# All low-part subtractions of the expert weights and of the second network's output weights on one engine

## The chip, the cores and the metric

The kernel runs on 1 core of a Trainium2 chip. The metric is the device time of one execution in microseconds (us). Five engines work side by side, each through its own queue in order: PE (TensorE, matrix products), DVE (VectorE), ACT (ScalarE), POOL (GpSimd) and SP (SyncE, which here only issues transfers).

## The reference, cut to what matters

Three stages in a row, all in float32: attention with global tokens, a mixture of experts with one expert per token, and a gated network with a convolution of three taps.

```python
def _moe_ref(x, w_gate, w_local, w1, w2):            # x: 4 x 576 x 512, 8 experts
    ...
            h = np.maximum(x[b, s] @ w1[e], 0.0)     # w1: 8 x 512 x 1024
            out[b, s] = p[e] * (h @ w2[e])           # w2: 8 x 1024 x 512

def _moe2_ref(x, w_in, conv_w, w_out):               # w_in: 512 x 1024, w_out: 1024 x 512
    h = np.maximum(x @ w_in, 0.0)
    ...
    gate = 1.0 / (1.0 + np.exp(-conv_out))
    return (h * gate @ w_out).astype(np.float32)
```

`moe2_w_in`, `moe2_conv_w` and `moe2_w_out` come as 64-bit floats and are made into 32-bit ones in the kernel.

## The kernel before, in words

Each product is taken as a sum of three, with both operands split in a high part (rounded to the format of PE) and a low part (the rest): high x high, high x low, low x high. So each weight matrix is needed twice, as `wh` and `wl`. For a piece of a matrix, `split_k` (lines 1018 to 1021) does this: ACT casts the staged piece `ws` to `wh` (L1020), and another engine subtracts, `wl = ws - wh` (L1021).

A set of tokens that go to one expert is cut into slots of 128. The loop `step` (L1274) works slot by slot: PE multiplies by the first matrix (`hp`, L1084, four row blocks of 128x1024), ACT applies the relu (`hs`, L1249), PE transposes (`hlp`, L1072), ACT and DVE split what was transposed into high and low (`xh` and `xl` for the tokens of the next slot, `gh` and `gl` for the hidden values, L1073 and L1077), and PE multiplies the hidden values of the slot before by the second matrix (`yp`, L1100, eight row blocks of 128x512). ACT copies the result (`ys`, L1253), and POOL scatters it to memory (L1057) and gathers the rows of a later slot (`xs`, L1045).

Where the next slot has another expert, `resplit` (L1268) splits the newly loaded matrix inside a branch that ACT, DVE and POOL take: the first matrix ahead of the next `hp`, the second matrix behind `gl`. SP loads the matrix after that into the stage as soon as the stage has been read (L1013). In the same steps a 64-bit weight of the second network is converted on DVE by seven integer operations (L987 to L992 and L994), with an exact integer addition on POOL between the last two (L993).

The last slot is written out by hand in `last` (L1186): its second matrix is split in two halves of four pieces; between them stand a small copy (`cw`, L1161) and a flag (`esi`, L939, L940), whose buffers PE needs for its transposes. Then the first rows of the second network are scaled on DVE (`fx`, L1333), transposed on PE (`f_tr`, L1340) and split (`f_x0h`, `f_x0l`, L1342 and L1343), interleaved with PE's `yp`, and the first matrix of the second network is split (`wl<-wf`). At the end of `run` (L1183) its second matrix is split: of eight pieces, DVE casts the odd ones (L1020) and ACT the even ones.

Behind that the second network runs per batch and block of 128 hidden values: PE `f` (L1408), ACT relu (`f_hp`, L1432), three taps on ACT and DVE (`fc`, L1425 and L1427), a sigmoid on ACT, the gate on POOL or DVE (`fg`, L1443), `fl` (L1456) on DVE, and the split of the transposed tokens of the next batch (`fxl`, L1375).

Which engine subtracts follows from four tables by the number of the piece: `POOL_K` for the splits in the loop (first matrix: piece 3; second matrix: pieces 1, 3, 5, 7) and for the first matrix of the second network, `POOL_L` for the last slot's second matrix, `POOL_F` for the second network's second matrix. Calls that name an engine, as the splits of the first two matrices during attention do (`nc.gpsimd`, 12 pieces), do not read the tables.

```python
def split_k(self, n, src, k, eng, cp=None):
    h, l = self.t[n][k]
    (cp.tensor_copy if cp else self.nc.scalar.copy)(h, src[n][:, k, :])
    eng.tensor_tensor(l, src[n][:, k, :], h.bitcast(F32), ALU.subtract)

def split(self, n, src, eng=None):
    for k in range(len(self.t[n])):
        self.split_k(n, src, k, eng or (self.nc.gpsimd if k in POOL_K[n] else self.nc.vector))
```

Of the kernel before, what the change touches and what calls it, by code (L numbers as in the profile page):

```python
# [973 lines left out]
SC_DVE = (0, 1, 2, 3)  # L974
PREP_F = ((3, 4, 5, 6), (1, 3, 5, 6), (1, 3, 5, 6))
PREP0 = {0: (0, 1, 12, 13), 3: (5, 2), 4: (6, 3), 5: (7, 4), 6: (8,), 7: (9,)}
POOL_L = (1, 3, 5, 7)
POOL_F = (1, 3, 5)
DVE_F = (1, 3, 5, 7)
POOL_K = {1: (3,), 2: (1, 3, 5, 7)}  # L980


def conv64(nc, raw, out):
# [13 lines left out]
class Weights:  # L997
# [25 lines left out]
# [5 lines that stand above are left out]
class Moe:  # L1028
# [134 lines left out]
    def run(self, cw6, cwr, cw, f2):  # L1163
# [19 lines left out]
        for k in range(NFC):  # L1183
            W.split_k(2, W.f, k, nc.gpsimd if k in POOL_F else nc.vector, nc.vector if k in DVE_F else None)

    def last(self, s, cwr, cw):  # L1186
# [6 lines left out]
        def split(a, b):  # L1193
            for k in range(a, b):
                W.split_k(1, W.f, k, nc.gpsimd if k in POOL_K[1] else nc.vector)

        def resplit(a, b):
            with self.tc.If(self.chg[s] != 0):
                for k in range(a, b):
                    W.split_k(2, W.s, k, nc.gpsimd if k in POOL_L else nc.vector)  # L1200

# [515 lines left out]
```

## Time and profile before

| what | value |
|---|---|
| median of 3 runs | 684.91 us (684.05 to 686.07) |
| the profiled execution | 682.78 us |
| its span, first to last instruction | 681.0 us |
| mean granted clock of PE | 0.976 of full speed |
| busy: PE, DVE, ACT, POOL | 617.3 us (91%), 435.8 us (64%), 332.6 us (49%), 271.1 us (40%) |
| subtractions `wl<-ws,wh` (L1021) on DVE | 49, 72.6 us in all |
| the same on POOL | 47, 83.0 us in all |

Attention and routing last to about 210 us of the span, the loop over the expert slots to about 450, the last slot to 472, and the second network to the end. A number such as 64% is a mean over these stages; what an engine's time is worth has to be read stage by stage. An engine is "idle before" an instruction when it waits, and the trace names what ended the wait.

### The profile page before, as it was taken

How to read it: one execution, taken by the hardware profiler on the slowest of the kernel's cores; microseconds unless marked ns; L12 is line 12 of the kernel's file. 1: busy time of each engine (PE TensorE's matmuls, PEld its weight loads, DVE VectorE, ACT ScalarE, POOL GpSimd, SP SyncE). 2: the span in 40 equal slices, each digit the busy share in tenths (PEclk: the TensorE clock that was granted, in tenths of full speed). 3: DMA queues.
4: the chain of work that ended last, by engine and by line, in shares of the span. 5: the costliest groups of instructions: out<-in, count | busy, mean ns of one | idle time of the engine just before them, and what ended most of it. 6: DMA issues, size and time to landing. Idle time of an engine off the chain costs nothing. (4 is left out here: it accounts for less than half of the span.)

```text
span 681.0 us, 15354 instructions
## 1 busy us (share of the span) xinstructions
PE 617.3 (91%) x5898; PEld 515.1 (76%) x5898; DVE 435.8 (64%) x824; ACT 332.6 (49%) x634; POOL 271.1 (40%) x281
## 2 busy tenths in 40 slices
PE   8777797787989999799999979986979999999997
PEld 7666675665768878687887868765978898898886
DVE  7866476674855677975767797567986366363340
ACT  5653448865124544452455444563655354363341
POOL 7583810038123545664455556333445142200200
PEclk9999898899799999999999999988979999999999
DMA  9997752354047465546336564321110010000001
GB/s 233 202 236 171 197 136 67 103 205 157 16 140 251 171 229 195 192 179 231 109 148 225 186 219 160 121 97 39 45 46 32 32 63 32 32 16 32 32 32 46
DMA packets 59354, 86.06 MB, mean 126 GB/s; under 512 B 25358, under 2 KB 33830, under 8 KB 59240
## 3 DMA queue, kind: packets, MB, share of 16 engines
q1 hardware_dynamic: 55752, 74.77, 35.3%
q0 software_dynamic: 3520, 10.23, 4.4%
q8 instruction: 48, 0.79, 0.5%
q14 instruction: 34, 0.28, 0.1%
HBM read 125.87 MB, written 15.79 MB: 208 GB/s over the span
## 5 line engine op out<-in xcount | busy, mean ns | idle before, releaser
L1427 DVE SCALAR_TENSOR_TENSOR fc<-f_hp,cw,fc 128x544 f32<-128x544 f32 (+2 forms) x66 | 57.4, 870 | 70.7 <-ACT fc L1425 69.4
L1021 POOL TENSOR_TENSOR wl<-ws,wh 128x512 fp32r<-128x512 f32 (+1 forms) x47 | 83.0, 1793 | 33.0 <-ACT wh L1020 17.1
L1021 DVE TENSOR_TENSOR wl<-ws,wh 128x512 fp32r<-128x512 f32 (+1 forms) x49 | 72.6, 1523 | 6.0 <-ACT wh L1020 5.9
L1100 PE MATMUL yp<-wh,gh 128*128 128x512 f32 x176 | 72.4, 411 | 1.1 <-ACTq L1271 1.1
L1100 PE MATMUL yp<-wl,gh 128*128 128x512 f32 x176 | 69.8, 397 | 0.1
L1100 PE MATMUL yp<-wh,gl 128*128 128x512 f32 x176 | 69.9, 397 | 0.0
L1020 ACT CAST wh<-ws 128x512 fp32r<-128x512 f32 (+1 forms) x96 | 66.1, 777 | 0.0
L1249 ACT ACTIVATE hs<-hp 128x512 f32<-128x512 f32 x44 | 24.3, 595 | 84.4 <-PE hp L1084 84.3
L1084 PE MATMUL hp<-wl,xh 128*128 128x512 f32 x176 | 57.0, 397 | 8.5 <-DVE wl L1021 6.8
L1084 PE MATMUL hp<-wh,xh 128*128 128x512 f32 x176 | 58.6, 405 | 0.7 <-ACT xh L1073 0.7
L1084 PE MATMUL hp<-wh,xl 128*128 128x512 f32 x176 | 56.0, 391 | 0.0
L1485 PE MATMUL f<-wh,fh 128*128 128x512 f32 (+1 forms) x144 | 55.5, 385 | 0.0
L1485 PE MATMUL f<-wl,fh 128*128 128x512 f32 (+1 forms) x144 | 55.0, 382 | 0.0
L1485 PE MATMUL f<-wh,fl 128*128 128x512 f32 (+1 forms) x144 | 55.0, 382 | 0.0
L1045 POOL DMA_INDIRECT xs<-x_dram,gidx x22 | 28.4, 1289 | 52.5 <-ACT pr L274 41.4
L1077 DVE TENSOR_TENSOR gl<-hlp,gh 128x512 fp32r<-128x512 f32 x44 | 28.5, 684 | 31.4 <-ACT gh L1073 27.3
L274 ACT ACTIVATE pr<-sp,nm 128x128 f32<-128x128 f32 x128 | 36.5, 375 | 24.4 <-DVE nm L271 24.4
L1057 POOL DMA_INDIRECT y_dram<-ys,sidx x22 | 25.6, 1165 | 56.5 <-ACT ys L1253 18.9
L1084 PEld LDWEIGHTS hp<-wl,xh 128*128 128x128 f32 x176 | 32.3, 188 | 19.0 <-DVE wl L1021 9.3
L993 POOL TENSOR_TENSOR wf<-wf,fx 128x512 int32<-128x512 int32 x16 | 20.7, 1296 | 62.9 <-DVE fx L992 62.9
L1253 ACT COPY ys<-yp 128x512 f32<-128x512 f32 x22 | 12.9, 586 | 61.2 <-PE yp L1100 56.4
L1100 PEld LDWEIGHTS yp<-wh,gh 128*128 128x128 f32 x176 | 33.9, 192 | 7.9 <-ACTq L1271 1.4
(361 smaller groups left out, 1574.4 us busy)
## 6 DMA issues: line engine op xcount, KB each, us to landing
ws<-in_moe_w_dram SPq DMA_DIRECT2D x42, 2048.0 KB
fx<-y_dram SPq DMA_DIRECT2D x17, 256.0 KB
x_dram<-x SPq DMA_DIRECT2D x16, 256.0 KB
fx<-in_moe_w_in_dram SPq DMA_DIRECT2D x8, 512.0 KB
fx<-in_moe_w_out_dram SPq DMA_DIRECT2D x8, 512.0 KB
out_dram<-fy SPq DMA_DIRECT2D x16, 256.0 KB
VA<-in_v_l_dram SPq DMA_DIRECT2D x20, 192.0 KB
raw<-in_q_l_dram SPq DMA_DIRECT2D x3, 1024.0 KB
```

The source lines that it names most:

```text
L274: nc.scalar.activation(pr[:, hp, :], sp[:, hp, :], AF.Exp, bias=nm[:, hp:hp + 1], scale=-1.0)
L993: nc.gpsimd.tensor_tensor(a, a, lo, ALU.add)
L1020: (cp.tensor_copy if cp else self.nc.scalar.copy)(h, src[n][:, k, :])
L1021: eng.tensor_tensor(l, src[n][:, k, :], h.bitcast(F32), ALU.subtract)
L1045: self.nc.gpsimd.indirect_dma_start(out=xs, out_offset=None, in_=self.x_dram[0:n, :], in_offset=bass.IndirectOffsetOnAxis(ap=self.rt.gidx[ ...
L1057: self.nc.gpsimd.indirect_dma_start(out=self.y_dram[:, :], out_offset=bass.IndirectOffsetOnAxis(ap=self.rt.sidx[:, s:s + 1], axis=0), in_= ...
L1077: self.nc.vector.tensor_tensor(hl[1][:, a:a + 4], t, hl[0][:, a:a + 4].bitcast(F32), ALU.subtract)
L1084: self.nc.tensor.matmul(hp[c], a[:, k, :], b[:, 512 * c:512 * c + 512], start=k == 0 and m == 0, stop=k == NKC - 1 and m == 2)
L1100: self.nc.tensor.matmul(yp, a[:, k, :], b, start=k == 0 and m == 0, stop=k == NFC - 1 and m == 2)
L1249: self.nc.scalar.activation(hs[:, 512 * c:512 * c + 512], hp[c], AF.Relu)
L1427: nc.vector.scalar_tensor_tensor(c[:, a:b], hp[:, a + t:b + t], self.cw[:, t, f:f + 1], c[:, a:b], ALU.mult, ALU.add)
L1485: self.nc.tensor.matmul(yp[:, cs], x[:, c], w[:, cs], start=f == 0 and n == 0, stop=f == NFC - 1 and n == 2)
```

## The change

All tables that name POOL become empty, so all these subtractions go to DVE, in the order of the pieces. Casts, matrix products, loads and branches stay.

```diff
-POOL_L = (1, 3, 5, 7)
-POOL_F = (1, 3, 5)
+POOL_L = ()
+POOL_F = ()
 DVE_F = (1, 3, 5, 7)
-POOL_K = {1: (3,), 2: (1, 3, 5, 7)}
+POOL_K = {1: (), 2: ()}
```

On DVE, in a step of the expert loop, before: from the branch behind `gl` to the first operation of the conversion (`ws_2711` is the stage of the second matrix, the number behind `wl_` the piece).

```order
L1271 COMPARE_AND_BRANCH
L1021 TENSOR_TENSOR wl_0_2721<-ws_2711,wh_0_2720 128x512
L1021 TENSOR_TENSOR wl_2_2725<-ws_2711,wh_2_2724 128x512
L1021 TENSOR_TENSOR wl_4_2729<-ws_2711,wh_4_2728 128x512
L1021 TENSOR_TENSOR wl_6_2733<-ws_2711,wh_6_2732 128x512
L1271 UNCONDITIONAL_BRANCH x2
L987 TENSOR_SCALAR wf_3947<-fx 128x512
```

The same place on DVE now:

```order
L1271 COMPARE_AND_BRANCH
L1021 TENSOR_TENSOR wl_0_2721<-ws_2711,wh_0_2720 128x512
L1021 TENSOR_TENSOR wl_1_2723<-ws_2711,wh_1_2722 128x512
L1021 TENSOR_TENSOR wl_2_2725<-ws_2711,wh_2_2724 128x512
L1021 TENSOR_TENSOR wl_3_2727<-ws_2711,wh_3_2726 128x512
L1021 TENSOR_TENSOR wl_4_2729<-ws_2711,wh_4_2728 128x512
L1021 TENSOR_TENSOR wl_5_2731<-ws_2711,wh_5_2730 128x512
L1021 TENSOR_TENSOR wl_6_2733<-ws_2711,wh_6_2732 128x512
L1021 TENSOR_TENSOR wl_7_2735<-ws_2711,wh_7_2734 128x512
L1271 UNCONDITIONAL_BRANCH x2
L987 TENSOR_SCALAR wf_3947<-fx 128x512
```

Four pieces have come from POOL's queue into DVE's, ahead of the conversion. The first matrix has the same form: its piece 3, which POOL did, now stands behind pieces 0 to 2.

On DVE, in the last slot, from the second half of the second matrix to the first rows of the second network (the difference; `wf_3947` holds the second network's first matrix):

```order
 L1198 COMPARE_AND_BRANCH
 L1021 TENSOR_TENSOR wl_4_2729<-ws_2711,wh_4_2728 128x512
-L1021 TENSOR_TENSOR wl_6_2733<-ws_2711,wh_6_2732 128x512
+L1021 TENSOR_TENSOR wl_5_2731<-ws_2711,wh_5_2730 128x512
+L1021 TENSOR_TENSOR wl_6_2733<-ws_2711,wh_6_2732 128x512
+L1021 TENSOR_TENSOR wl_7_2735<-ws_2711,wh_7_2734 128x512
 L1198 UNCONDITIONAL_BRANCH x2
 L1333 TENSOR_SCALAR fx<-fx,gate 32x512
 L1333 TENSOR_SCALAR fx<-fx,gate 128x512
 L1021 TENSOR_TENSOR wl_2_2717<-wf_3947,wh_2_2716 128x1024
+L1021 TENSOR_TENSOR wl_3_2719<-wf_3947,wh_3_2718 128x1024
```

Two pieces more stand ahead of the two scalings that PE's transposes need, and one large piece more behind them.

On DVE, at the end of `run`, the split of the second network's second matrix (the difference; `wf_3948` holds that matrix):

```order
 L1021 TENSOR_TENSOR wl_0_2721<-wf_3948,wh_0_2720 128x512
 L1020 CAST wh_1_2722<-wf_3948 128x512
+L1021 TENSOR_TENSOR wl_1_2723<-wf_3948,wh_1_2722 128x512
 L1021 TENSOR_TENSOR wl_2_2725<-wf_3948,wh_2_2724 128x512
 L1020 CAST wh_3_2726<-wf_3948 128x512
+L1021 TENSOR_TENSOR wl_3_2727<-wf_3948,wh_3_2726 128x512
 L1021 TENSOR_TENSOR wl_4_2729<-wf_3948,wh_4_2728 128x512
 L1020 CAST wh_5_2730<-wf_3948 128x512
+L1021 TENSOR_TENSOR wl_5_2731<-wf_3948,wh_5_2730 128x512
 L1021 TENSOR_TENSOR wl_6_2733<-wf_3948,wh_6_2732 128x512
 L1020 CAST wh_7_2734<-wf_3948 128x512
```

Each of the three moved pieces now stands right behind the cast that it reads.

## Rows read from the trace of the kernel before

**Rows 1.** Stretches (us): busy us of PE, PEld, DVE, ACT, POOL; granted clock; DMA share.
```profile
210.00:450.00 240.00, 229.97 (x1103) 186.79 (x1101) 169.47 (x221) 113.39 (x191) 122.02 (x82) 1.00 0.51 181
472.00:500.00 28.00, 24.47 (x185) 24.02 (x185) 27.34 (x33) 17.93 (x31) 13.44 (x15) 0.93 0.26 72
```
**Rows 2.** Waits of PE, 210 to 450 us: total us, times, longest.
```profile
PE hp L1084 <- DVE wl L1021: 6.8, 6, 1.7
PE hp L1084 <- DVEq L1271: 1.7, 4, 0.4
PE hlp L1072 <- DVE xl L1077: 1.6, 6, 0.3
```
**Rows 3.** Waits of PE, 450 to 472 us.
```profile
PE f L1408 <- PEq L1173: 4.0, 1, 4.0
PE hlp L1072 <- DVE esi L939: 2.0, 1, 2.0
PE f_tr L1340 <- DVE fx L1333: 1.5, 2, 1.0
PE f_tr L1340 <- issue: 1.2, 1, 1.2
```
**Rows 4.** Waits of PE, 472 to 500 us.
```profile
PE f_tr L1373 <- DVE fxl L1375: 3.5, 2, 3.0
```
**Rows 5.** Timeline of DVE, 268 to 288 us: start, length, instruction, count, idle before.
```profile
268.36 1.29 DVE L1077 TENSOR_TENSOR gl<-hlp,gh 128x512 fp32r<-128x512 f32 x2 [3.35 <-ACT gh L1073]
269.56 0.68 DVE L1021 TENSOR_TENSOR wl<-ws,wh 128x512 fp32r<-128x512 f32 x1
270.40 4.96 DVE L1021 TENSOR_TENSOR wl<-ws,wh 128x512 fp32r<-128x512 f32 x3 [0.15 <-ACT wh L1020]
275.27 1.52 DVE L987 TENSOR_SCALAR wf<-fx 128x512 int32<-128x512 int32 x1
...
281.53 5.67 DVE L1021 TENSOR_TENSOR wl<-ws,wh 128x1024 fp32r<-128x1024 f32 x3
```
**Rows 6.** Timeline of POOL, 268 to 288 us.
```profile
269.93 6.58 POOL L1021 TENSOR_TENSOR wl<-ws,wh 128x512 fp32r<-128x512 f32 x4 [0.81 <-ACT wh L1020]
...
282.55 2.44 POOL L1021 TENSOR_TENSOR wl<-ws,wh 128x1024 fp32r<-128x1024 f32 x1
```
**Rows 7.** Timeline of DVE, 212 to 219 us.
```profile
212.88 3.50 DVE L1021 TENSOR_TENSOR wl<-ws,wh 128x1024 fp32r<-128x1024 f32 x3 [0.25 <-ACT wh L1020]
```
**Rows 8.** Groups of POOL by shape, 210 to 450 us: count, busy us, mean ns, idle.
```profile
L1021 POOL TENSOR_TENSOR wl<-ws,wh 128x512 fp32r<-128x512 f32 x24 | 39.4, 1676 | 4.8 <-ACT wh L1020 4.8
...
L1021 POOL TENSOR_TENSOR wl<-ws,wh 128x1024 fp32r<-128x1024 f32 x7 | 18.5, 2639 | 19.2 <-PE yp L1100 15.6 <-ACT wh L1020 3.3
```
**Rows 9.** Page, costliest groups: the casts on ACT.
```profile
L1020 ACT CAST wh<-ws 128x512 fp32r<-128x512 f32 (+1 forms) x96 | 66.1, 777 | 0.0
```
**Rows 10.** Timeline of DVE, 472 to 486 us.
```profile
472.88 0.42 DVE L1020 CAST wh<-wf 128x512 fp32r<-128x512 f32 x1
...
473.81 1.50 DVE L1020 CAST wh<-wf 128x512 fp32r<-128x512 f32 x1
```
**Rows 11.** Timeline of PE, 282 to 289 us.
```profile
282.80 0.72 PE L1084 MATMUL hp<-wl,xh 128*128 128x512 f32 x2 [1.52 <-DVE wl L1021]
...
286.12 0.74 PE L1084 MATMUL hp<-wl,xh 128*128 128x512 f32 x2 [1.69 <-DVE wl L1021]
```
**Rows 12.** Timeline of DVE, 449 to 468 us.
```profile
450.71 2.76 DVE L1021 TENSOR_TENSOR wl<-ws,wh 128x512 fp32r<-128x512 f32 x1 [0.34 <-ACT wh L1020]
...
457.32 1.43 DVE L1021 TENSOR_TENSOR wl<-ws,wh 128x512 fp32r<-128x512 f32 x1 [0.27 <-ACT wh L1020]
458.67 4.00 DVE L1333 TENSOR_SCALAR fx<-fx,gate 32x512 f32<-32x512 f32 x2
```
**Rows 13.** Two stretches behind long waits, columns as in rows 1.
```profile
455.00:458.00 3.00, 3.00 (x9) 2.33 (x9) 2.65 (x4) 2.85 (x6) 1.15 (x1) 0.55 0.71 230
500.00:505.00 5.00, 5.00 (x23) 5.00 (x24) 4.83 (x6) 1.68 (x3) 2.22 (x3) 0.50 0.07 27
```

## The prediction

> **What bounds the kernel now.** I read the stretches first, then the waits of the tensor engine (PE) in each, then the two queues that end those waits. Between 210 and 450 us, the expert loop, PE is busy for 229.97 of 240 us [rows 1]: the stretch lasts as long as PE's own work, plus 10 us in which PE stands still. All of these 10 us are waits for DVE [rows 2]: 6.8 us for the low parts `wl` of the first weight matrix, 1.7 us for DVE's branch behind the split, 1.6 us for `xl`, which is queued behind the same split. In the last slot and the way out (450 to 472 us) PE waits for DVE again: 2.0 us for the flag `esi`, queued behind a split, then 1.5 and 1.2 us for the scaled rows `fx` [rows 3]. From 472 to 500 us DVE is busy for 27.34 of 28 us [rows 1] and PE waits 3.5 us for its `fxl` [rows 4]. So in all three stretches what PE lacks is DVE.
>
> The next question is why DVE is late. While POOL is idle, a subtraction of a 128x512 piece takes 0.68 us [rows 5], and two short operations in a row take 1.29 us, so one every 0.61 us. Beside POOL's four the next three take 4.96 us, which is 1.65 each, and POOL's four take 6.58 us [rows 5, 6]. For 128x1024 pieces three in a row on DVE take 3.50 us while POOL stands [rows 7], but 5.67 us where POOL subtracts too; the 2.2 us between them is nearly the whole 2.44 us of POOL's one piece, from 282.55 to 284.99 us [rows 5, 6]. The step of the integer conversion behind the split (L987) takes 1.52 us and ends at 276.79 us, just behind POOL's last piece (269.93 + 6.58 = 276.51). So while POOL does a two-input operation, DVE's operations on these buffers stand still, and the sharing gives no parallel work.
>
> **The change, part by part.** It moves 24 + 7 = 31 subtractions in the loop [rows 8] and 8 behind it (four of the last slot's second matrix, one 128x1024 and three 128x512 of the second network) from POOL to the place in DVE's queue given by their chunk number. The twelve that the code hands to POOL by name, around 148 to 171 us, stay. POOL keeps its branches, gathers and scatters; they come earlier, and PE waits for none of them. SP gets its load of the next expert earlier, since its buffer is free sooner; the casts never waited for a load (0.0 us idle before 96 of them [rows 9]), so this gains nothing and costs nothing.
>
> Second matrix, 8 pieces of 128x512: before, from 269.56 to 276.51 us on both engines, 6.95 us. Now 0.68 + 7 x 0.61 = 4.95 us on DVE, ending at 274.5. L987, a one-input operation, then takes about what a cast of this size takes, 0.42 us [rows 10], and ends at 274.9 and not 276.8. Everything behind it on DVE moves up by 1.9 us: `xl`, the branch, and the first-matrix split.
>
> First matrix, 4 pieces of 128x1024: alone 1.14 us apart, the last 1.22 long. The first now starts at 281.53 - 1.9 = 279.6 and is done at 280.85. PE wanted it at 282.80 - 1.52 = 281.28 [rows 11], or 281.0 once its wait for `xl` of 0.3 has gone: just in time. The second is done at 282.0; PE wanted it at 286.12 - 1.69 = 284.43, in the new timing 282.6. The third and fourth end at 283.1 and 284.3; PE asks one piece per 1.6 us (284.43 - 282.80), so at 284.2 and 285.8. No wait is left.
>
> **Term A, the loop.** This pattern (both matrices change) comes twice and has 2 x (1.5 + 1.7) of the 6.8 us; two changes of the first matrix alone have the remaining two waits of 0.2, which fall as the piece behind POOL does. The four waits of 0.4 for the branch and the six of 0.3 for `xl` are ended by the 1.9 us. All 16 go: 10.1 us; I leave 0.1 for the tight place. **A = 10.0**. At least 3.7 (only the waits during which POOL itself holds DVE: 2 x 1.7 + 2 x 0.2), at most 10.1, since PE's own work stays.
>
> **Term B, last slot.** DVE's second piece of the first half takes 2.76 us [rows 12], held by two of POOL's: 2.1 us over its own 0.68. Two pieces more take 1.2, but fill the 0.34 us of idle time ahead of it: 1.2 us gained. In the second half, of 0.75 us freed (1.43 - 0.68) and an idle 0.27, two more pieces take 1.2: a loss of 0.2. The two scalings take 4.00 us [rows 12], held by two more of POOL's pieces; at a cast's 0.42 each, 3.1 us come free, and the 128x1024 piece that follows costs 1.1. Sum 1.2 - 0.2 + 3.1 - 1.1 = 3.0. **B = 3.2**, with 0.2 for a shorter time at the low clock there [rows 13]. At least 1.3, at most the 4.7 us that PE waits; 4.0 us at the exit, where all engines wait for the last scatter, stay.
>
> **Term C, into the second network.** Three casts on DVE take 1.5 us and not 0.42, held by POOL's three pieces [rows 10]: 3.2 us come free, and the three pieces themselves cost about 0.7 each, since each now reads the cast before it. Net 1.1 us earlier at `fc`, and DVE is the bound from there to 500 us, so PE's 3.5 us shrink. **C = 1.0**; at worst 2.1 us the other way, if the freed casts bring nothing, at best 3.5. Here a rule speaks against the change. The Trainium skill, Perfetto Trace Analysis, section Optimizing Scalar/DVE Operations, says that where DVE is saturated, giving work to GPSIMD may make sense, though it warns that the shared port may eat the gain. By that advice the three pieces taken back, at 0.68 us each, would make this place 2 us longer and the time 684.9 - 10.0 - 3.2 + 2.0 = 673.7; the casts held to 1.5 us show that here its warning counts.
>
> Sum: 10.0 + 3.2 + 1.0 = 14.2 us. The profiled execution took 682.78 us, 2.1 below the median of 684.91, so I expect a profile of 668.6 and a **median of 670.7 us**.
>
> **Rivals.** *Only the direct holds go.* If DVE's chain behind the second-matrix split is not earlier (its raw data or `xh` late), the loop gives 3.7, B 1.3, C 0: 684.9 - 5.0 = 679.9. Against it: `xl` and L987 follow DVE's own work without idle time. 14%.
>
> *More, through the clock.* The granted clock is 0.55 at 455 to 458 us and 0.50 at 500 to 505 us [rows 13], the lower level of 1.2 GHz for most of it, each time behind PE's longest idle stretches (2.0 and 3.0 us). If shorter waits keep it at 2.4 GHz, up to 3.0 x 0.45 + 5.0 x 0.5 = 3.9 us more: 666.8. For it: waits of 1.5 and 1.7 us in the loop left the clock at 1.00 [rows 1]. Against: DVE stays the bound at 500 us and part of the wait remains. 8%.
>
> *DVE becomes the bound: slower.* If DVE's long pieces are slow of themselves (ACT casts from the same buffer at that time) and not held by POOL, eight on DVE take 8 x 1.65 = 13.2 us where both engines took 6.95, and PE waits up to 6.2 us more behind each of the six second-matrix changes in the loop (24 pieces on POOL, four each): 684.9 + 37 = 722. It decides from 6.95 / 8 = 0.87 us a piece. Against: 0.68 for the piece that starts before POOL does, and 3.50 for three large ones while POOL stands. 4%. In this case the page's advice to unload a full DVE, and not its warning, would be right.
>
> *Nothing to measure*: another wait, such as ACT's, takes the place of each. ACT is busy for 113 of 240 us [rows 1], so 2%.
>
> **How the numbers follow.** The forecast has 72%. A measurement of this kernel can tell about 0.3%, 2 us, from no change. Faster by more: 72 + 14 + 8 = 94%; within: 2%; slower: 4%. The likeliest case runs from 668 to 674 (A down to 8, B 1.3 to 4.7, C 0 to 2). The range of 666.5 to 676.5 takes in the clock's case and an A that loses half; it leaves out most of the case of the direct holds and the slow one.
>
> **What would show it.** Right: no subtraction on POOL after 172 us; DVE's 128x512 pieces near 0.68 us each and 128x1024 near 1.22; PE's waits from 210 us on down from 10 us to under 1; the exit some 13 us earlier. B is wrong if PE still waits over 1.5 us for `fx`; C if `fxl` still costs 3.5. The whole is wrong if DVE's pieces stay over 0.87 us without POOL beside them.

## The result and the profile after

The changed kernel takes 668.28 us (median of 4 runs, 667.00 to 669.74) where the kernel before took 684.48 in the same comparison (4 runs, 684.01 to 686.07): a ratio of 0.976, interval 0.9734 to 0.9786. The forecast was 670.7 us, range 666.5 to 676.5. The profiled execution took 667.0 us, its span is 665.2.

The page of the changed kernel, busy time by engine and the group of the subtractions:

```profile
span 665.2 us, 15266 instructions
PE 617.4 (93%) x5898; PEld 517.8 (78%) x5898; DVE 421.7 (63%) x863; ACT 331.8 (50%) x634; POOL 199.0 (30%) x242
...
L1021 DVE TENSOR_TENSOR wl<-ws,wh 128x512 fp32r<-128x512 f32 (+1 forms) x84 | 66.7, 862 | 4.5 <-ACT wh L1020 4.4
```

DVE does 39 instructions more than before and is busy for 14 us less (421.7 against 435.8). Its subtractions in this group rose from 49 to 84 and their time fell from 72.6 to 66.7 us; POOL lost 72 us of busy time. PE's own work is the same, 617.4 us.

One step of the loop, DVE's timeline from 262 to 284 us (start, length, instruction, count, idle before), the place of [rows 5]:

```profile
268.68 1.29 DVE L1077 TENSOR_TENSOR gl<-hlp,gh 128x512 fp32r<-128x512 f32 x2 [4.36 <-ACT gh L1073]
269.89 4.89 DVE L1021 TENSOR_TENSOR wl<-ws,wh 128x512 fp32r<-128x512 f32 x8
274.70 0.42 DVE L987 TENSOR_SCALAR wf<-fx 128x512 int32<-128x512 int32 x1
...
279.89 4.62 DVE L1021 TENSOR_TENSOR wl<-ws,wh 128x1024 fp32r<-128x1024 f32 x4
```

Eight pieces take 4.89 us on DVE alone (4.95 in the forecast); two engines together took 6.95. The operation behind them is back from 1.52 to 0.42 us. Four large pieces take 4.62 us, where three took 5.67.

The waits of PE: from 210 to 437 us there is none left, where [rows 2] add up to 10.1 us. In the last slot and the way out (437 to 456.8 us; total, times, longest), the place of [rows 3]:

```profile
PE f L1408 <- PEq L1173: 3.9, 1, 3.9
PE f_tr L1340 <- DVE fx L1333: 1.7, 2, 0.9
PE hlp L1072 <- ACT hs L1249: 0.7, 1, 0.7
PE yp L1100 <- ACT gh L1073: 0.2, 1, 0.2
```

and from 456.8 to 490 us one wait of 2.7 for `fxl`, where [rows 4] have two with 3.5 in all. To see where the time went, I cut both spans at the same instructions: the second copy of a result on ACT (`ys`, L1253), the last but one of these copies, the first `f` (L1408) on PE behind the way out, the fifth block of `f_tr` (L1373), and the end. The marks of before are 204.01, 448.54, 471.74 and 499.90 us, those of after 205.97, 437.03, 456.75 and 485.13 us.

| stretch, us | before | after | difference | forecast |
|---|---|---|---|---|
| start to second `ys` (none of the moved work) | 204.01 | 205.97 | +1.96 | 0 |
| expert loop | 244.53 | 231.06 | -13.47 | -10.0 (A) |
| last slot and way out | 23.20 | 19.72 | -3.48 | -3.2 (B) |
| first `f` to fifth `f_tr` | 28.16 | 28.38 | +0.22 | |
| from there to the end | 181.11 | 180.10 | -1.01 | -1.0 (C, both) |
| span | 681.01 | 665.23 | -15.78 | -14.2 |

The first line is no effect of the change: with the same code up to there, other profiles of this study have 203.2 to 209.3 us. The -1.01 of the last stretch is none either, as the part on term C shows. The loop gave 3.5 us more than the forecast, so the experiments ask first whether that is the loop's own, and then whether POOL really holds DVE.

### The profile page after: what moved, and what is told of

The parts are those of the page before. It is cut to its first block, busy times and chain, and to the rows that moved or that the text cites. A ratio compares the mean times of both kernels' runs of the same rounds, so it can differ in the third digit from the quotient of the medians.

```text
span 665.2 us, 15266 instructions
## 1 busy us (share of the span) xinstructions
PE 617.4 (93%) x5898; PEld 517.8 (78%) x5898; DVE 421.7 (63%) x863; ACT 331.8 (50%) x634; POOL 199.0 (30%) x242
## 5 line engine op out<-in xcount | busy, mean ns | idle before, releaser
L1021 DVE TENSOR_TENSOR wl<-ws,wh 128x512 fp32r<-128x512 f32 (+1 forms) x84 | 66.7, 862 | 4.5 <-ACT wh L1020 4.4
L1253 ACT COPY ys<-yp 128x512 f32<-128x512 f32 x22 | 12.9, 587 | 61.2 <-PE yp L1100 56.5
L1432 ACT ACTIVATE f_hp<-f 128x544 f32<-128x544 f32 x31 | 19.4, 627 | 42.4 <-PE f L1408 42.3
```

## The experiments

The kernel before, run beside them on the same chips, took 684.66 us (beside the first four), 685.87 (beside the two with added work on POOL) and 684.64 (beside the last three). In the first three T1 says that each stretch gave what the table shows, T2 that part of the loop's gain came from elsewhere; the fourth has a rival of its own.

**Loop tables alone** (`POOL_L`, `POOL_F` as before):

```diff
-POOL_K = {1: (3,), 2: (1, 3, 5, 7)}
+POOL_K = {1: (), 2: ()}
```

> Only the table of the expert loop is emptied (it also moves the one 128x1024 piece of the second network's first matrix); the last slot's second matrix and the second network's second matrix stay shared with POOL. Theory 1 (POOL holds DVE, and each of PE's 16 stops costs what lies between the starts of two products, 13.5 us in all): about 684.5 - 13.5 = 671.0 us. Theory 2 (the stops cost only the idle time that the trace lists, 10.1 us, and the rest of the gain comes from the places behind the loop): about 674.4 us.

671.18 us (670.40 to 672.61, 4 runs), ratio 0.9798, interval 0.9763 to 0.9834. By the same marks its loop takes 231.17 us, 13.36 less than before: T1. Its last slot takes 22.28 us, 0.92 less, since `POOL_K` also moves the second network's piece 3: the first matrix alone, below, moves that piece too and has 22.11 us there, the second matrix alone does not and has 23.05.

**Only behind the loop:**

```diff
-POOL_L = (1, 3, 5, 7)
-POOL_F = (1, 3, 5)
+POOL_L = ()
+POOL_F = ()
```

> The other half: only the last slot's second matrix and the second network's second matrix move to DVE, the loop stays shared. Theory 1: 3.0 to 4.0 us, so 680.5 to 681.5 us. Theory 2: the rest of the 16 us, 6 us, so 678.5 us.

679.41 us (673.58 to 683.38, 10 runs), ratio 0.9924, interval 0.9890 to 0.9957; this lies between the two, so the median does not decide. Its trace does: loop 244.72 us (before 244.53), last slot 21.11 (2.09 less). Nothing of the loop's gain comes from behind it.

**Only the second matrix in the loop, and only the first:**

```diff
-POOL_K = {1: (3,), 2: (1, 3, 5, 7)}
+POOL_K = {1: (3,), 2: ()}
```
```diff
-POOL_K = {1: (3,), 2: (1, 3, 5, 7)}
+POOL_K = {1: (), 2: (1, 3, 5, 7)}
```

> In the loop only the second matrix moves to DVE; piece 3 of the first matrix stays on POOL. Theory 1: everything queued behind the second-matrix split on DVE comes 1.9 us earlier, so the waits for xl, for the branch and for the first piece of the first matrix go (start to start 2.8 + 2.4 + 3.4 = 8.6 us), but the waits behind POOL's own piece 3 stay: about 676 us. Theory 2: 1.6 + 1.7 + 3.0 = 6.3 us by listed idle time: 678.2 us.

> In the loop only piece 3 of the first matrix moves to DVE; the second matrix stays shared. Theory 1: the four waits during which POOL's piece holds DVE go, 2 x 1.85 + 2 x 0.36 = 4.4 us start to start: 680.1 us; the waits of 1.5 us for the first piece, and those for xl and the branch, stay. A rival, that one more piece of 1.14 us in DVE's queue delays what follows: no gain, 684.5 us.

678.27 us (668.92 to 681.66, 6 runs), ratio 0.9857, interval 0.9797 to 0.9917; and 679.21 us (672.10 to 682.59, 9 runs), 0.9902, interval 0.9858 to 0.9946. The waits of PE from 210 us to the end of the loop, with the second matrix alone on DVE:

```profile
PE hp L1084 <- DVE wl L1021: 4.9, 2, 3.3
```

and with the first matrix alone on DVE:

```profile
PE hp L1084 <- DVE wl L1021: 3.0, 2, 1.5
PE hp L1084 <- DVEq L1271: 2.0, 4, 0.7
PE hlp L1072 <- DVE xl L1077: 1.6, 6, 0.3
```

This separates the two ways of waiting. With the second matrix on DVE, the waits for `xl` and for the branch are gone: they were DVE's chain behind that split. Two waits remain behind POOL's one large piece. With the first matrix on DVE, the second wait of each pair (1.7) and the small ones (0.2) are gone, and the chain is late as before. The loops take 237.84 and 239.89 us, 6.69 and 4.64 less; together 11.3, less than the 13.5 of both. From one `ys` to the next, the first step in which both matrices change takes 16.51 us before, 14.52 with the second matrix alone on DVE, 14.58 with the first alone and 12.60 with both: there the halves add up. In the other step of this kind the second matrix alone takes 17.44 us, more than the 16.52 before. This one step loses 2.9 us against the first; the small stops of 0.2, which go in either half, give 1.0 back.

In that step PE's wait is 3.3 us, longer than any in the loop before. POOL's piece (394.39 to 396.73 us) meets DVE's first large piece there, which takes 4.14 us, and not its second, as it does in the first such step; and TensorE's granted clock falls behind the wait (DVE's row, then two stretches, columns as in [rows 1]):

```profile
393.69 6.41 DVE L1021 TENSOR_TENSOR wl<-ws,wh 128x1024 fp32r<-128x1024 f32 x3 [0.24 <-issue]
```
```profile
392.00:398.00 6.00, 2.74 (x17) 2.06 (x16) 5.01 (x3) 2.13 (x4) 5.65 (x4) 1.00 0.97 371
398.00:401.00 3.00, 3.00 (x8) 2.35 (x9) 3.00 (x4) 0.00 (x0) 0.71 (x1) 0.50 0.24 92
```

At 1.2 in place of 2.4 GHz for 3 us, eight products start there, and the step costs 4.85 us over the same step of the changed kernel (between two `ys`), 1.6 more than the wait; the first such step costs 1.92 for a wait of 1.65, so some 1.3 of the 1.6 are the clock's. Had this step gone as the first, the second matrix alone would stand at about 675.4 us, near T1's 676. That is an estimate from one profile: the median as it is lies at T2's number, so the waits decide here and not the median. Whether the other runs had such a step is not recorded; one took 668.92 us at a mean clock of 0.978, the others have 0.960 to 0.967. The median of the first matrix alone lies 0.9 us below T1's 680.1, and 5.3 from its rival's 684.5.

**Work on POOL that shares no data.** The changed kernel, with eight operations on a scratch tile of POOL's own beside each split of a second matrix in the loop; they only add work. In the one kernel with two inputs, in the other with one. (The tile is 128x256 because the kernel has no room left for one of 128x512, with which the same pair was first planned.)

```diff
+        self.j = hl.tile([P, 256], F32, name="junk")
+        nc.gpsimd.memset(self.j, 0.0)
...
+        if eng is None and n == 2:
+            for _ in range(8):
+                self.nc.gpsimd.tensor_tensor(self.j, self.j, self.j, ALU.subtract)
```
```diff
-                self.nc.gpsimd.tensor_tensor(self.j, self.j, self.j, ALU.subtract)
+                self.nc.gpsimd.tensor_scalar(self.j, self.j, 1.0, None, ALU.mult)
```

> The changed kernel (668.3 us) with 48 added two-input subtractions on POOL, eight beside each of the six second-matrix splits in the loop, on a 128x256 scratch tile that nothing else reads or writes. Nothing is left out. T1, POOL's two-input operation holds DVE whatever data it works on: each DVE operation that meets one lasts until that one ends, so DVE's pieces of 128x512 go from 0.69 to over 1 us while POOL works, and PE waits for wl, xl and the branch again: 3 to 12 us more in the loop, 671 to 680 us. T2, the hold comes from the raw buffer that both engines read or from chunks that they take in turn: DVE's pieces stay at 0.69 us and the time within 1 us of 668.3.

> The same with 48 one-input multiplications on POOL on the 128x256 scratch tile in place of the two-input ones. Nothing is left out. T1, any POOL operation holds DVE: as with the two-input ones, 671 to 680 us. T2, only an operation with two inputs holds DVE entirely, one with one input slows it partly or not at all: DVE's 128x512 pieces stay under 1.0 us, 668 to 670 us.

685.64 us (681.53 to 688.82, 10 runs), ratio to before 0.9986, interval 0.9949 to 1.0024: the whole gain is lost, more than T1 expected. And 670.50 us (668.94 to 674.45, 4 runs), ratio 0.979, interval 0.9731 to 0.985. In these two kernels L1023 is the former L1021, and lines behind L1029 are 5 higher. POOL and DVE beside each other with two inputs:

```profile
274.97 7.78 POOL L1030 TENSOR_TENSOR junk<-junk 128x256 f32<-128x256 f32 x8
...
275.39 7.91 DVE L1023 TENSOR_TENSOR wl<-ws,wh 128x512 fp32r<-128x512 f32 x8
283.22 0.41 DVE L987 TENSOR_SCALAR wf<-fx 128x512 int32<-128x512 int32 x1
```

and with one:

```profile
267.88 9.18 POOL L1030 TENSOR_SCALAR junk<-junk 128x256 f32<-128x256 f32 x8
...
268.28 5.73 DVE L1023 TENSOR_TENSOR wl<-ws,wh 128x512 fp32r<-128x512 f32 x8
...
275.19 0.64 DVE L989 TENSOR_SCALAR fx<-fx 128x512 int32<-128x512 int32 x1
```

With two inputs DVE finishes one piece per operation of POOL (eight in 7.91 us beside eight in 7.78) and is free again when POOL is, though the two share no data: T1, the hold needs no common buffer and no taking of turns by data. POOL is held as well: its operations last 0.62 us at the shortest and 0.94 us in the middle (shortest, median, longest in ns):

```profile
L1030 POOL TENSOR_TENSOR junk<-junk x48: 623/942/954, 235.9 to 429.5; 128x256 f32<-128x256 f32 x48
```

With one input POOL works longer (9.18 us), but DVE's eight pieces take only 5.73 us: 0.84 us more than alone, so T2, partly slowed. With the conversion behind the split slowed too, the first-matrix split starts 11.37 us behind the second's (268.28 to 279.65), in the changed kernel 10.00 (269.89 to 279.89). That is enough to bring back a wait of 1.4 us for `wl` twice, and smaller ones for the branch. The waits of PE from 200 to 455 us, with two inputs:

```profile
PE hlp L1077 <- DVE xl L1082: 7.7, 6, 1.3
PE hp L1089 <- DVE wl L1023: 3.0, 2, 1.5
PE hp L1089 <- DVEq L1276: 1.7, 4, 0.4
```

The loop takes 247.24 us with two inputs and 236.15 with one. Of the 247.24 some 1.6 are the clock's. Two steps have the same two stops, 1.27 us for `xl` and 1.5 for `wl`; behind one pair the clock falls, behind the other it does not (two stretches of the one step, one of the other; columns as in [rows 1]):

```profile
403.00:408.00 5.00, 2.22 (x14) 1.42 (x13) 4.12 (x8) 1.66 (x3) 2.91 (x3) 1.00 0.87 319
408.00:411.00 3.00, 3.00 (x8) 2.32 (x9) 3.00 (x3) 0.00 (x0) 1.81 (x1) 0.50 1.04 408
```
```profile
290.00:293.00 3.00, 3.00 (x15) 2.49 (x14) 3.00 (x4) 0.00 (x0) 1.59 (x1) 1.00 1.05 407
```

The step with the low clock takes 17.15 us, the other 15.53.

**Farther in the same direction.** The changed kernel once more as the base; the gate products of the second network all on DVE (before, only those of its second half); and, on top, the twelve subtractions of the attention stage:

```diff
-                st[n - 1] = self.gates(*st[n - 1], self.nc.vector if n > NFC else self.nc.gpsimd)
+                st[n - 1] = self.gates(*st[n - 1], self.nc.vector)
```
```diff
-                m.W.split_k(1, m.W.s, k, nc.gpsimd)
+                m.W.split_k(1, m.W.s, k, nc.vector)
...
-                    m.W.split_k(2, m.W.s, k, nc.gpsimd)
+                    m.W.split_k(2, m.W.s, k, nc.vector)
```

> The changed kernel once more, as the base for the two variants beside it: 668.3 us, 667 to 670.

> The changed kernel with all of the second network's gate products (fg, two-input, 128x544) on DVE; before only those of its second half. T1, POOL's two-input operations hold DVE here too: the second of each pair of fc operations goes from 1.74 to about 0.9 us, the product itself costs DVE 0.62, so each block's chain on DVE is 0.2 to 0.35 us shorter; with five blocks before PE's stop at 485 us (2.72 us) that stop shrinks by 1 to 2 us and the time is 665.5 to 667.5 us. Rival: fc is long of itself (ACT writes into the same tile): DVE has 0.62 us more per block, PE's stop grows by up to 3 us, 669 to 671 us.

> As e7_gates, and the twelve low parts around 148 to 171 us, in the attention stage, on DVE too: no two-input operation on large pieces is left on POOL there. PE stands still for 4.6 us in all between 140 and 175 us and waits there for ACT's softmax and the routing, not for wl. DVE is busy for about half of that stretch. T1: as e7_gates within 1 us, up to 1 us less if the routing's DVE operations at 169 us come earlier. Rival: the twelve (4 x 1.14 + 8 x 0.61 = 9.4 us of DVE) delay the attention's own operations on DVE that PE needs, 2 to 5 us slower than e7_gates.

The base took 665.55 us (663.67 to 672.34, 6 runs; ratio 0.9742, interval 0.9686 to 0.9797), the gates on DVE 664.95 (663.45 to 667.61, 6 runs; 0.9718, 0.9672 to 0.9764), all three 671.26 (669.39 to 673.39, 6 runs; 0.9815, 0.9769 to 0.9861).

With the gates on DVE, DVE is relieved as T1 says. In the changed kernel a pair of `fc` beside POOL's product (467.69 us, 1.47 long) reads:

```profile
467.16 2.58 DVE L1427 SCALAR_TENSOR_TENSOR fc<-f_hp,cw,fc 128x544 f32<-128x544 f32 x2 [0.99 <-ACT fc L1425]
```

and with the gates on DVE:

```profile
469.41 0.72 DVE L1443 TENSOR_TENSOR fg<-f_hp,fc 128x544 f32<-128x544 f32 x1
...
471.08 1.67 DVE L1427 SCALAR_TENSOR_TENSOR fc<-f_hp,cw,fc 128x544 f32<-128x544 f32 x2 [0.95 <-ACT fc L1425]
```

But DVE now waits for ACT's `fc` ahead of each pair (0.95, later 0.24 us), and PE's stop at 485 us only shrinks from 2.73 to 2.47 us. The 0.6 us between the medians can't be told from nothing: the expected 1 to 2 us did not come.

The attention stage is the counter-example: 6.3 us slower than with the gates alone, so the rival came true, by more than its 2 to 5 us. PE's waits there, 144 to 200 us:

```profile
PE op L296 <- ACT pr L274: 3.3, 1, 3.3
PE ptp L282 <- ACT pr L274: 2.1, 1, 2.1
PE ptp L282 <- ACT pts L284: 1.4, 1, 1.4
```

in the base, where no wait for `pr` or `pts` is longer:

```profile
PE op L296 <- ACT pr L274: 1.3, 1, 1.3
```

and DVE's timeline with the twelve on DVE:

```profile
151.53 0.69 DVE L1077 TENSOR_TENSOR xl<-hlp,xh 128x512 fp32r<-128x512 f32 x1 [0.61 <-ACT xh L1073]
152.48 1.22 DVE L1021 TENSOR_TENSOR wl<-ws,wh 128x1024 fp32r<-128x1024 f32 x1 [0.26 <-ACT wh L1020]
153.62 0.68 DVE L271 TENSOR_REDUCE nm<-sp 128x4 f32<-128x512 f32 x1
```

In the base the next row maxima `nm` (L271) come right behind `xl` (148.07, then 148.67 us). Here a `wl` stands between them in DVE's queue and waits for ACT's cast of its piece; ACT's softmax `pr` waits for `nm`, and PE for `pr`. This is no hold but a queue in order, and POOL was the better place for these twelve. From ACT's first cast of these pieces to the first `ys`, this kernel's profile takes 39.3 us, the ten others 35.3 to 37.4: the traces show 2 to 4 of the 6.3 us there, the rest in no place.

## Why the prediction was right, and where it was off

**What bounds, and the hold.** Right. DVE's pieces take 0.61 us each without POOL's, and the run with unrelated work shows that POOL's two-input operation itself is the cause; the prediction had said "on these buffers", which is narrower than what holds. Every duration that the forecast built on came out: 4.89 us for 4.95, L987 0.42, the four large pieces 4.62 (three pitches of 1.14 and 1.22 make 4.64), the first of them from 279.89 us for 279.6.

**"Just in time."** Right. DVE's first large piece ends at 281.11 us (279.89 + 1.22) and PE takes it at 281.16; the two steps of this kind still take 12.59 and 12.60 us where others take 12.29, so 0.3 us are left in each, too short to be listed as a wait. The one-input run shows the same: 1.4 us more on DVE, and PE waits there for 1.4.

**Term A, 10.0 us: mis-sized, measured 13.5.** All 16 listed waits went, as said. The step that failed is "at most 10.1, since PE's own work stays": it took the idle time in [rows 2] for the whole price of the waits. Steps from `ys` to `ys` show the price: stops of 0.26 and 0.42 us cost 1.18 (13.47 against 12.29 in the changed kernel), stops of 0.27, 1.52 and 1.69 us cost 3.91 (16.51 against 12.60). The records say where the rest hides. PE's timeline of the kernel before, without a stop and behind one:

```profile
277.03 0.39 PE L1100 MATMUL yp<-wh,gl 128*128 128x512 f32 x1
277.25 0.39 PE L1100 MATMUL yp<-wh,gh 128*128 128x512 f32 x1
...
283.37 0.62 PE L1084 MATMUL hp<-wh,xl 128*128 128x512 f32 x2
283.82 0.61 PE L1084 MATMUL hp<-wh,xh 128*128 128x512 f32 x2
```

A product is recorded 0.39 us long but the next starts 0.23 us later; the last one before a stop shows its full 0.39, so 0.16 us of each stop is booked as busy. The transposes `hlp` behave alike (0.60 us for four, 0.27 for one, so 0.11 apart: again 0.16). And the first two products behind the stop of [rows 11] take 283.37 - 282.80 = 0.57 us until the next, where two take 0.45 (283.82 - 283.37): 0.12 more. Sixteen times 0.16 and ten times 0.12 (the stops that are not transposes) make 3.8; measured are 13.47 - 10.1 = 3.4. That this explains the difference is worked out from the records, not tried by itself. The other variants bear out that each stop costs about 0.2 us more than is listed: to the changed kernel's 231.0 us, 12 stops of 6.6 us in all add 8.9 (first matrix alone), 6 of 4.1 add 5.1 (one input), and 12 of 12.4 add 14.6 besides the clock's 1.6 (two inputs).

**Term B, 3.2 us: right (3.5), by its own items.** The timeline of DVE in the last slot of the changed kernel:

```profile
438.17 2.50 DVE L1021 TENSOR_TENSOR wl<-ws,wh 128x512 fp32r<-128x512 f32 x4 [4.14 <-ACT wh L1020]
...
443.39 2.49 DVE L1021 TENSOR_TENSOR wl<-ws,wh 128x512 fp32r<-128x512 f32 x4
445.80 0.86 DVE L1333 TENSOR_SCALAR fx<-fx,gate 32x512 f32<-32x512 f32 x2
446.59 2.34 DVE L1021 TENSOR_TENSOR wl<-wf,wh 128x1024 fp32r<-128x1024 f32 x2
...
449.06 0.47 DVE L1333 TENSOR_SCALAR fx<-fx,gate 128x512 f32<-128x512 f32 x1
```

Counted from the mark at the slot's start, the first half is through 1.3 us earlier (forecast 1.2), the scalings start 1.4 us earlier (the second half costs nothing, forecast a loss of 0.2) and fall from 4.00 to 0.86 us (3.1, as forecast), and the second large piece costs 1.1 (as forecast): 3.4 us, and the slot's last `ys` comes 3.4 us earlier, 16.30 for 19.67 us behind the mark. The exit gives the other 0.1.

The sign of an error that the prediction named came all the same: PE still waits 1.7 us for `fx`, and its listed waits shrank by only 2.2 us (8.7 to 6.5). What PE waits for does not measure the slot here, because the clock hides part of it. Before, the slot has 3 us at 0.55 of the clock [rows 13]. The second matrix alone has the kernel's old code in this slot, and the full clock there (its stretch at the same place, 6.46 us behind its mark of 444.42, and its wait for `fx`):

```profile
450.88:453.88 3.00, 2.98 (x12) 2.10 (x12) 2.84 (x4) 3.00 (x6) 1.38 (x2) 1.00 0.57 197
```
```profile
PE f_tr L1340 <- DVE fx L1333: 2.3, 2, 1.8
```

It reaches the last `ys` after 19.49 us, the kernel before after 19.67: PE's products are done sooner, and PE waits 0.8 us longer for `fx`. The loop tables alone (0.50 of the clock there) and the first matrix alone (1.00) are a second such pair, 18.55 and 18.52 us. So the low clock costs this slot 0.2 us at most; the 0.2 that the prediction gave it was enough, and DVE's chain accounts for all of the gain but 0.1.

**Term C, 1.0 us: the mechanism is right, but nothing of it is in this pair.** DVE's split is through earlier, as worked out: it ends 7.3 us behind PE's restart (456.75 to 464.02; before 8.4).

```profile
463.33 0.69 DVE L1021 TENSOR_TENSOR wl<-wf,wh 128x512 fp32r<-128x512 f32 x1
```

Whether PE gains from it hangs on the clock at the restart. Its first 5 us in the changed kernel, in the kernel before and in the kernel with two-input work on POOL:

```profile
456.75:461.75 5.00, 5.00 (x22) 5.00 (x23) 4.37 (x9) 2.06 (x4) 0.00 (x0) 0.50 0.49 146
```
```profile
471.74:476.74 5.00, 5.00 (x29) 5.00 (x30) 4.47 (x6) 2.36 (x5) 2.99 (x2) 0.70 0.48 121
```
```profile
476.05:481.05 5.00, 5.00 (x28) 5.00 (x29) 4.36 (x9) 2.25 (x5) 0.00 (x0) 0.66 0.42 121
```

| profiles | the three pieces on | clock, first 5 us | DVE idle for ACT's `fc` | restart to fifth `f_tr` |
|---|---|---|---|---|
| before; first matrix alone | POOL | 0.70; 0.70 | none | 28.16; 28.37 |
| loop tables; second matrix alone | POOL | 0.53; 0.50 | none | 28.34; 28.35 |
| two inputs; one input | DVE | 0.66; 0.66 | none | 27.28; 27.32 |
| changed kernel again | DVE | 0.51 | 0.72 | 27.98 |
| changed kernel; only behind the loop | DVE | 0.50; 0.50 | 0.99; 0.95 | 28.39; 28.42 |

Where the clock is back early, the earlier DVE brings 0.8 to 1.1 us, as forecast; at 0.50, ACT's relu waits longer for PE's first products (3.75 us in the changed kernel, 2.75 with two inputs), its `fc` comes late, DVE stands idle, and 0 to 0.4 us are left. The 1.01 us behind the fifth `f_tr` are the clock too: the kernel before runs its first 7 us there at 0.60, the changed one at 0.76, and the loop tables and the second matrix alone, with the three pieces on POOL, also have 0.76 and take 180.16 us from there to the end, against 180.10 of the changed kernel. The Trainium skill (Perfetto Trace Analysis, section Optimizing Scalar/DVE Operations) says that where DVE is saturated, giving work to GPSIMD may make sense, but that a move between these two might not help, since they share a port. By the advice the three pieces would better have stayed on POOL; the table shows nothing lost by taking them back, and with the clock back early a gain, as by the warning. That the cause is a port is shown by no run.

**The rivals.** The direct holds alone (679.9) fell: the waits of the chain went too. Slow pieces of DVE itself (722) fell at 0.61 us a piece. The clock's rival has nothing that the change can be shown to have given: in the last slot the low clock is gone but cost 0.2 us at most, and at 485 to 490 us it still falls (0.65), behind the wait of 2.7 us that stays; the 1.0 us less there is found without the moved pieces too.

**The sum.** 14.2 forecast, 17.7 by the stretches: 13.5 and 3.5 for A and B, 0.8 for the rest, which is the clock's and not C's. Of the 17.7, 2.0 are hidden in this pair of profiles by the opening. The medians differ by 16.2 us, on another chip by 19.1. That the forecast of the time came out within 2.4 us is in part luck: A was 3.5 us too small and C's 1.0 was not there.

## What to carry to other kernels

Before work is shared between DVE and POOL, compare the duration of one DVE operation with POOL idle and with POOL busy in the same trace: if DVE's operation lasts as long as POOL's, sharing two-input work adds nothing, as here, and delays all that is queued behind. Take such work back where DVE's chain ends the wait; leave it on POOL where DVE's queue would have to wait for another engine's result ahead of something urgent. And price a stop of PE by start-to-start times, not by listed idle time: here each of the 16 stops cost 0.2 us more than listed, a third of 10.1 us in all. A wait that is left, or a low clock, tells nothing by itself where another engine's chain sets the time: compare two kernels with the same code there.

## What was not expected of the hardware

- POOL's operation with two inputs holds DVE on unrelated data until POOL is through (DVE 7.91 us beside 7.78) and is itself held (0.94 us for 0.62); one with one input holds DVE only in part (DVE 5.73 us beside 9.18; alone 4.89). Why one input matters less is not shown.
- A single wait of 3.3 us of PE inside the loop was followed by 3 us at half the granted clock, while the kernel before has pairs of 1.5 and 1.7 us at the full clock [rows 1, 11]. But the length of the wait does not settle it: with two-input work on POOL, stops of 1.27 and 1.5 us were followed by 3 us at 0.50 in one step and by none in the other. What decides is open.
- Profiles of the same code (save the clearing of a scratch tile) differ by up to 6 us before any of the moved work, 203.2 to 209.3 us; what sets this is open.
